# A new order for the head of a hand-written plan: batch 0's second slice and batch 1's last transposed weights ahead of the third slice of G

## The chip, the core and the metric

The kernel runs on one NeuronCore of a Trainium2 chip. The core has five engines with instruction streams of their own: TensorE (PE; its weight loads are a row of their own, PEld), VectorE (DVE), ScalarE (ACT), GpSimd (POOL) and SyncE (SP, which only issues transfers). They meet through semaphores. Transfers run on 16 shared DMA engines; SP, ACT and POOL issue them. The metric is the device time of one execution in microseconds, the median of several runs.

## What is computed

Eight batches of eight heads. Each head has 512 tokens `x` and 32 `state` rows, 64 numbers each. The tokens attend to the states and the states to the tokens; both results, heads side by side, go through a feed-forward layer with a three-way maximum.

```python
scores = scale * np.matmul(x, state.transpose(0, 1, 3, 2))
a = np.exp(scores - scores.max(-1, keepdims=True))
a /= a.sum(-1, keepdims=True) + 1e-09
xread = np.matmul(a, state)
# sread: the same with state and x exchanged
attn = np.concatenate([xread, sread], axis=2)      # 8 x 8 x (512+32) x 64
x = attn.transpose(0, 2, 1, 3).reshape(4352, 512)
h = np.maximum(np.maximum(x @ w1, x @ w2), x @ w3)  # w1, w2, w3: 512 x 768
out = h @ w_out                                     # 768 x 512
```

## The kernel before

**The algebra.** For the tokens of batch b, `xread @ w` is never formed through `xread`. The states of the batch are first multiplied with the three weight matrices, which gives G (line 363: 256 rows of head and state by 3 x 768 columns), and then the attention weights are multiplied with G. So per batch there are: the scores (`sc`), their exponentials (`ex`), row sums (`sum`), the normalised weights `a` (`wt`), their transpose `aT` (`at` and `atc` on TensorE and a copy, or `atd`, a DMA transpose), G in slices (`g`, or runs of columns `gr`) with its evacuation from PSUM to SBUF (`gc`, `grc`), the first layer (`l1`, six blocks m of 128 hidden columns, each with three PSUM banks, one for each of w1, w2, w3, two matmuls into each, line 416), the three-way maximum (`m0` on ACT copies the first bank, `ma` and `mb` on DVE take the maximum with the second and third), and the second layer (`l2`, line 447) with its evacuation (`l2c`) and stores (`so`). `sr` and `srs` are the states' own reading of the tokens and its scaling; `pad` lays x out for it.

**Order.** Nothing is scheduled automatically. A plan of short operations, written out as text, is walked through once, and each operation appends its instructions to the streams of its engines. Within an engine the order of the plan is the order of execution; between engines semaphores hold. `FIRST` holds the head (batches 0 and 1 and the beginning of batch 2), `EACH` one period for batches 2 to 6 with batch numbers relative to the period's, `LAST` the end. The letters behind an operation choose its engine: A ACT, D DVE, P POOL, S SP; `AD` gives one half to each.

**Loads.** `lst k` loads the states of batches 2k and 2k+1; `stc` casts them, `stt` transposes them on TensorE, `stp` places them into the block-diagonal tile `bds[k]`. `lxg b g` loads half of the heads of x of batch b through POOL, which casts on the way; `lxu` loads without a cast (through SP), and `cxu` casts. `lw m0 m1 i` loads columns 128 m0 to 128 m1 of weight matrix i (line 179), `lwo` the output weights (line 184). Slice m of G (`g b m`) needs columns 128 m to 128 m + 128 of all three matrices. `ones` on POOL first copies a number out of the output weights (line 194), so it waits for them. `xtd b` (line 249) is SP's DMA transpose of x for the scores; batches 0 and 1 are transposed on TensorE instead (`xt`, then `xtc`).

**PSUM.** There are four single banks (`BANKS` gives the bank of each use in the plan's order) and two pairs (`PAIRS`). A product may start when the last reader of its bank is done. A slice of G takes a pair, a block of `l1` three of the four single banks.

**Fillers.** `busy n` issues n matmuls of zeros (line 211) that nobody reads. They stand in the head, where TensorE would otherwise wait.

**The part around the change**, TensorE's order before, from the first slices of G on:

```
at 0 0; sr 0; busy; at 0 1; g 0 0; busy; g 1 0; sr 1; at 1 0; g 1 1; g 0 1; l1 0 0; g 1 2; g 0 2; busy;
at 1 1; l1 0 1; l1 0 2; l1 1 0; l1 1 1; g 0 3; g 1 3; stt 1; l1 1 2; g 0 5; g 0 4; l1 0 3; g 1 4;
gr 2 ..; l1 1 3; l1 0 5; gr 2 ..; g 1 5; l1 1 4; gr 2 ..; gr 2 ..; l1 0 4; stt 2; sc 2; l2 0 3; l2 0 1;
```

Of the kernel before, what the change touches and what calls it, by code (L numbers as in the profile page):

```python
# [17 lines left out]
FIRST = """  # L18
    lst 0 A; lxu 0 0 S; zero; clr 0; clr 1; clr 2; clr 3; warm; lxg 0 1; busy 1; xones 1; ident; busy 1;
    lxg 1 0; busy 1; busy 1; stc 0 D; busy 1; busy 1; busy 1; busy 1; busy 1; lxg 1 1; stt 0; busy 2;  # L20
    cxu 0 0 D; xt 0 0; stp 0 A; busy 1; xt 0 1; busy 1; xtc 0 0 D; lw 0 2 1; lw 0 2 2; xtc 0 1 D;
    busy 1; sc 0 0; busy 1; lw 0 1 0; busy 1; sc 0 1; lw 1 3 0; ex 0 0; busy 1; busy 1; xt 1 0; sum 0 0;
    lw 2 3 1; busy 1; ex 0 1; sum 0 1; xt 1 1; busy 1; xtc 1 0 AD; busy 1; lw 2 3 2; busy 1; xtc 1 1 A;
# [14 lines left out]
"""
EACH = """
    pad 1; gr 1 1792 2304; gr 1 0 512; grc 1 1792 2304 AD; l2 -1 0; l2 -1 1; l1 0 0; grc 1 0 512 D;  # L40
    l2c -1 0 A; m0 0 0; sc 1 -; l2 -1 3; gr 1 1024 1280; ex 1 -; xtd 2; gr 1 1280 1792; l2c -1 1 D;
    ma 0 0; gr 1 512 1024; mb 0 0; sr 1; grc 1 1024 1280 A; l1 0 1; l1 0 2; sum 1 -; l1 0 3; srs 1;
    l1 0 5; l2c -1 3 A; m0 0 1; m0 0 2; ma 0 1; mb 0 1; ma 0 2; m0 0 3; mb 0 2; srt -2; ma 0 3;
    wt 1 - P; m0 0 5; mb 0 3; l2 -1 2; grc 1 1280 1792 A; grc 1 512 1024 A; ma 0 5; mb 0 5; l2c -1 2 D;
    l1 0 4; so -1 2 4 P; m0 0 4; ma 0 4; lx 3; mb 0 4; atd 1; ap -2 A; so -1 0 2 P;
"""
LAST = """
    srt 6; l1 7 0; srt 7; l2 6 0; l1 7 2; m0 7 0; l1 7 3; l1 7 4; ap 7 D; m0 7 2; srt 5; ap 6 A; ma 7 0;
    m0 7 3; mb 7 0; ap 5 A; l2c 6 0 D; ma 7 2; l2 6 1; l1s 0; l2 6 2; m0 7 4; mb 7 2; l1 7 1; l2c 6 1 A;
    ma 7 3; m0 s 0; l2c 6 2 A; l1s 2; l1 7 5; ma 7 4; mb 7 4; look; ma s 0; m0 7 1; m0 s 2; mb s 0;  # L50
    so 6 2 3 S; m0 7 5; mb 7 3; l1s 1; ma 7 1; mb 7 1; ma s 2; mb s 2; ma 7 5; m0 s 1; ma s 1; l1s 5;
    so 6 0 1 S; mb 7 5; l2p 7 2 384 512; l1s 3; m0 s 5; ma s 5; mb s 1; m0 s 3; mb s 5;
    l2pc 7 2 384 512 A; l2p 7 0 384 512; l2p 7 3 256 512; sop 7 2 384 512 P; ma s 3; l2p 7 2 128 384;
    mb s 3; l2p 7 0 0 128; l2pc 7 0 0 128 A; l2pc 7 3 256 512 D; l2p 7 1 0 128; l2p 7 3 0 256;
    l2pc 7 0 384 512 D; flag; l2pc 7 1 0 128 A; l2pc 7 2 128 384 A; l1s 4; m0 s 4; l2 6 3;
    sop 7 0 0 128 P; ma s 4; sop 7 0 384 512 P; mb s 4; l2p s 0 256 512; so 6 1 2 P; l2 s 1;
    sop 7 3 256 512 A; l2c 6 3 D; l2p 7 2 0 128; sop 7 1 0 128 S; l2p s 0 0 256; so 6 3 4 A;
# [18 lines left out]
def kernel(  # L76
# [41 lines left out]
    st = [data.tile([128, 4, 2, D], BF16, name=f"st{k}") for k in range(B // 2)]  # L118
# [97 lines left out]
    def states_cast(k, c):  # L216
        copier[c](out=st[k], in_=st_f[k].unsqueeze(2).to_broadcast((128, 4, 2, D)))
# [326 lines left out]
    def perform(plan, base=0):  # L544
        for op in plan.replace("\n", " ").split(";"):
# [132 lines left out]
```

## Time and profile before

| | |
|---|---|
| median of 3 runs | 153.05 us (152.54 to 153.25) |
| the profiled execution, first to last instruction | 151.4 us |
| TensorE busy | 146.4 us, 97% |
| VectorE, ScalarE, GpSimd busy | 118.9, 82.8, 57.0 us |
| fillers on TensorE (line 211) | 27, 10.0 us |
| DMA | 22.29 MB, mean 147 GB/s |

The median lies 1.65 us above the span; that is what lies around the first and the last instruction, and the difference between executions. All times of a profile are counted from the span's first instruction. A busy TensorE isn't TensorE at its peak: matmuls are pipelined and their ends are modelled, so that a group of six that takes 1.3 us at the rate of its starts is shown with up to 1.47 us. A row of a timeline gives the start, the length, the engine, the line, the operation and its tiles, the number of instructions that were merged, and in brackets the idle time of the engine ahead of it with what ended it. `SPq` and `ACTq` rows are issues of transfers.

### The profile page before, as it was taken

What the parts mean: (1) busy time and instruction counts of PE and PEld (TensorE: products, weight loads), DVE (VectorE), ACT (ScalarE), POOL (GpSimd) and SP (SyncE); (2) the same over time, 40 slices, a digit from 0 to 9 for tenths busy, and PEclk for the clock granted to TensorE, in tenths of its full rate; (3) what the DMA queues carried; (4) which work ended last, traced back from release to release, by engine and by line L of the source; (5) the groups of instructions that cost most, each with busy time, mean ns of one, the idle gap of its engine ahead of it and who ended that gap; (6) DMA issues with size and microseconds to landing.
All of it is one profiled execution on the core that took longest, in us unless ns stands there. A gap on an engine that the chain in (4) does not pass through costs nothing.

```text
span 151.4 us, 3635 instructions
## 1 busy us (share of the span) xinstructions
PE 146.4 (97%) x1431; PEld 73.8 (49%) x1431; DVE 118.9 (79%) x204; ACT 82.8 (55%) x143; POOL 57.0 (38%) x79
## 2 busy tenths in 40 slices
PE   6999799999999999999999999999999999999992
PEld 2566343335445443544354435443544446679771
DVE  6477698999977898879987988798879887675353
ACT  3368558976364665466646664666466653331220
POOL 6979650561528505540554046414331200001500
PEclk9999999999999999999999999999999999999999
DMA  3999999979737979999589749974503250300455
GB/s 115 211 189 195 207 198 195 151 149 139 139 74 167 230 59 265 129 223 132 155 124 230 144 130 140 232 122 141 218 0 78 68 226 4 122 18 17 175 180 196
DMA packets 39108, 22.29 MB, mean 147 GB/s; under 512 B 23072, under 2 KB 36896, under 8 KB 39088
## 3 DMA queue, kind: packets, MB, share of 16 engines
q0 software_dynamic: 15872, 13.96, 48.7%
q1 hardware_dynamic: 21776, 6.82, 23.4%
q10 hardware_dynamic: 1440, 1.25, 2.7%
q8 instruction: 12, 0.20, 0.5%
q14 instruction: 8, 0.07, 0.2%
HBM read 15.20 MB, written 8.91 MB: 159 GB/s over the span
## 4 chain that ended last, share of the span: by engine, by line
PE 86%; DMA 6%; POOL 4%; issue 1%; DVE 1%; POOLq 0%
PE pw L416 46%; PE po L447 25%; DMA w<-in_moe_w_dram 6%; PE pg L363 5%; PE po L462 4%; POOL w L179 2%; PE ps L262 2%; PE psr L327 2%; POOL x L168 1%; PE pgh L363 1%; PE pt L222 1%; DVE held L522 0%; PE idle L520 0%; PE idle L211 0%; DVE osb L466 0%
## 5 line engine op out<-in xcount | busy, mean ns | idle before, releaser
L416 PE MATMUL pw<-aT,G 128*128 128x512 bf16 x288 | 66.8, 379 | 0.0
L431 ACT CAST t<-pw 128x512 bf16<-128x512 f32 (+1 forms) x54 | 30.4, 564 | 28.9 <-PE pw L416 27.2
L416 PEld LDWEIGHTS <-G 128*128 128x128 bf16 x288 | 27.2, 98 | 33.2 <-issue 1.9
L436 DVE TENSOR_TENSOR t<-t,pw 128x512 bf16<-128x512 bf16 (+1 forms) x54 | 35.4, 655 | 9.5 <-ACT t L431 7.4
L447 PE MATMUL po<-wout,ht 128*128 128x512 bf16 x168 | 39.9, 379 | 0.0
L440 DVE TENSOR_TENSOR ht<-t,pw 128x512 bf16<-128x512 bf16 x48 | 32.9, 687 | 4.3
L447 PEld LDWEIGHTS <-ht 128*128 128x128 bf16 x168 | 15.3, 98 | 19.0 <-issue 1.7
L284 POOL TENSOR_TENSOR a<-e,rden 128x1024 bf16<-128x1024 bf16 (+1 forms) x9 | 14.5, 1620 | 24.1 <-ACT osb L454 11.1
L477 POOL DMA_DIRECT2D out_dram<-osb x13 | 7.4, 572 | 30.5 <-ACT t L431 27.5
L403 ACT CAST G<-pg 128x1024 bf16<-128x1024 f32 (+1 forms) x17 | 14.3, 875 | 1.3 <-PE pg L363 1.3
L311 POOL COPY xp<-x 128x1024 bf16<-128x1024 bf16 x12 | 12.3, 1062 | 5.5 <-DMA x<-in_x_dram 5.5
L454 DVE COPY osb<-po 128x512 f32<-128x512 f32 x16 | 10.9, 684 | 2.4 <-PE po L447 2.3
L276 DVE TENSOR_REDUCE seen<-e 128x32 f32<-128x1024 bf16 (+1 forms) x10 | 10.0, 999 | 3.6 <-ACT e L269 3.6
L403 DVE CAST G<-pg 128x1024 bf16<-128x1024 f32 (+1 forms) x13 | 12.2, 972 | 0.7 <-ACT G L403 0.7
L454 ACT COPY osb<-po 128x512 f32<-128x512 f32 x13 | 7.7, 593 | 8.9 <-PE po L447 8.9
L269 ACT ACTIVATE e<-ps 128x1024 bf16<-128x1024 f32 (+1 forms) x10 | 8.5, 854 | 6.6 <-PE ps L262 6.4
L363 PE MATMUL pg<-w,bd 64*32 64x512 bf16 (+1 forms) x288 | 10.8, 362 | 0.9 <-DMA w<-in_moe_w_dram 0.9
L211 PE MATMUL idle<-zero 128*128 128x512 bf16 x27 | 10.0, 477 | 1.3 <-DVE zero L187 1.3
L472 POOL DMA_DIRECT2D out_dram<-osb x4 | 2.2, 544 | 19.4 <-ACT osb L466 19.4
L381 ACT CAST G<-pg 128x768 bf16<-128x768 f32 x9 | 7.1, 801 | 3.3 <-PE pg L363 3.1
L416 PE MATMUL pw<-atp,w 128*128 128x256 bf16 x72 | 8.7, 272 | 0.0
L416 PEld LDWEIGHTS <-w 128*128 128x128 bf16 x72 | 6.9, 98 | 1.5
(70 smaller groups left out, 116.0 us busy)
## 6 DMA issues: line engine op xcount, KB each, us to landing
out_dram<-osb POOLq DMA_DIRECT2D x12, 512.0 KB, 3.5
x<-in_x_dram POOLq DMA_DIRECT2D x4, 512.0 KB, 7.3
x<-in_x_dram POOLq DMA_DIRECT2D x7, 256.0 KB, 5.5
w<-in_moe_w_dram POOLq DMA_DIRECT2D x4, 256.0 KB, 7.5
w<-in_moe_w_dram POOLq DMA_DIRECT2D x2, 384.0 KB, 7.9
wout<-in_moe_w_out_dram POOLq DMA_DIRECT2D x1, 768.0 KB, 11.6
out_dram<-osb SPq DMA_DIRECT2D x3, 256.0 KB, 2.4
osb<-in_x_dram SPq DMA_DIRECT2D x1, 512.0 KB, 4.0
```

The source lines that it names most:

```text
L211: nc.tensor.matmul(p, zero[:, 0:128], zero, start=True, stop=True)
L276: nc.vector.reduce_sum(out=den, in_=parity(e[b], g), axis=AX.X)
L284: times[c](out=parity(a[b], g).rearrange("p j g s n -> p j (g s) n"), in0=parity(e[b], g).rearrange("p j g s n -> p j (g s) n"), in1=rdens ...
L311: nc.gpsimd.tensor_copy(out=xp[b][:, :, :, g * (D + 1):g * (D + 1) + D], in_=v[:, g])
L363: nc.tensor.matmul(p(s, g), bd(b, 2 * s + g)[64 * g:64 * g + 64, g, :], f(w_sb[64 * g:64 * g + 64, s]), start=True, stop=True, tile_positi ...
L403: copier[c[g]](out=v[:, g:h], in_=p[:, g:h, 0:c1 - c0])
L416: nc.tensor.matmul(pw[i][:, 0:n], lhs(i, k), rhs(k), start=(k == 0), stop=(k == nk - 1))
L431: nc.scalar.copy(out=t0s[b, m][:, 0:n], in_=open_ps["l", b, m][0][:, 0:n])
L436: nc.vector.tensor_max(t1s[b, m][:, 0:n], t0s.pop((b, m))[:, 0:n], open_ps["l", b, m][1][:, 0:n])
L440: nc.vector.tensor_max(ht[b][:, m, :], t1s.pop((b, m))[:, 0:n], open_ps.pop(("l", b, m))[2][:, 0:n])
L447: nc.tensor.matmul(p, ht[b][:, m, j * 128:(j + 1) * 128], wout_sb[:, m, :], start=(m == 0), stop=(m == NM - 1))
L454: copier[c[i]](out=o[:, j, i * w:i * w + w], in_=p[:, i * w:i * w + w])
```

## The change

**Form.** `FIRST`, `EACH` and `LAST` become one `PLAN` that is written out for all batches. The buffers, which rotated before, are now named by a table (`PLACES`), in the order in which they rotated; a buffer is taken where it is first written. Two buffers hold the cast states instead of four. The four groups of tokens are kept in the order 0, 2, 1, 3 from the exponentials on (`turned`), and the second layer takes its columns accordingly. New functions for transposed scores (`sq`, `eq`, `etd`, `std`) exist but stand nowhere in the plan.

**Order.** From `gr 3 512 1024` on, TensorE's instructions stand in the same order as before, with the same banks but for the first few; so do those of VectorE from `sum 3`, ACT from `gr 3 ..`'s last evacuations, and the rest from batch 4's loads on. What differs is the head:

- TensorE: ten `busy` operations, eleven fillers, fewer. `at 1 1` and `l1 0 1` stand ahead of `g 0 2` and `g 1 2`. The blocks and slices behind them change places.
- ACT and DVE exchange evacuations: `xtc 0`, `gc 0 0`, `atc 1 1`, `gc 0 5`, the run 0 to 512 of batch 2, and batch 0's second-layer evacuations go to ACT; `stp 0`, `gc 0 1`, `wt 0 1`, `wt 2` to DVE; `gc 1 1`, `gc 0 4`, `gc 1 5` and the run 1792 to 2304 are halved between them.
- ACT issues `lst 1` and `lst 2` one behind the other, around `ex 1 1`; `lst 2` stood behind `m0 1 1`.
- POOL's loads of W come in the order `lw 0 2 1; lw 0 1 0; lw 0 2 2; lw 1 3 0; lw 2 3 2; lw 2 3 1; lw 3 6 1; wt 0 0; lw 3 4 0; lw 3 6 2; wt 1 0; wt 1 1; lw 4 6 0` (before `lw 0 2 1; lw 0 2 2; lw 0 1 0; lw 1 3 0; lw 2 3 1; lw 2 3 2; wt 0 0; wt 0 1; lw 3 4 0; lw 3 6 2; lw 3 6 1; lw 4 6 0; wt 1 1`). Behind them: `stc 1; lxg 2 0; lxg 2 1; lwo; stc 2; ones; pad 2; lxg 3 1; stc 3; lxg 3 0; pad 3; so 0 0` (before `stc 1; lxg 2 1; lxg 2 0; lwo; pad 2; ones; stc 2; lxg 3 1; lxg 3 0; stc 3; wt 2; so 0 0; lx 4; so 0 2; pad 3`).
- SP: `atd 2` stands ahead of `xtd 3`.

The core of the diff (of the plan, the part of the new head that the text speaks of):

```diff
-    busy 1; wt 0 0 P; wt 0 1 P; xones 0; sc 1 0; ex 1 0; busy 1; sc 1 1; at 0 0; atc 0 0 A; sr 0;
-    busy 1; sum 1 0; lw 3 4 0; at 0 1; lst 1 A; lw 3 6 2; lw 3 6 1; ex 1 1; wt 1 0 D; g 0 0; gc 0 0 D;
-    busy 1; sum 1 1; g 1 0; sr 1; atc 0 1 A; lw 4 6 0; wt 1 1 P; at 1 0; srs 0; g 1 1; g 0 1; stc 1 P;
-    l1 0 0; gc 1 1 D; gc 1 0 A; g 1 2; g 0 2; atc 1 0 A; busy 1; gc 0 1 A; m0 0 0; at 1 1; lxg 2 1;
-    srs 1; ma 0 0; l1 0 1; lxg 2 0; gc 0 2 A; l1 0 2; atc 1 1 D; l1 1 0; m0 0 1; m0 0 2; lwo; m0 1 0;
+    ex 1 0; busy 1; busy 1; sc 1 1; lst 1 A; lw 1 3 0; ex 1 1; lst 2 A; lw 2 3 2; lw 2 3 1; lw 3 6 1; wt 0 0 P;
+    wt 0 1 D; lw 3 4 0; at 0 0; sr 0; at 0 1; atc 0 0 A; sum 1 0; sum 1 1; lw 3 6 2; wt 1 0 P; g 0 0; g 1 0;
+    wt 1 1 P; sr 1; atc 0 1 A; gc 1 0 D; lw 4 6 0; at 1 0; srs 1; srs 0; gc 0 0 A; stc 1 P; lxg 2 0; lxg 2 1;
+    lwo; g 0 1; g 1 1; atc 1 0 A; l1 0 0; stc 2 P; ones; pad 2; at 1 1; m0 0 0; gc 0 1 D; ma 0 0; gc 1 1 AD;
+    atc 1 1 A; l1 0 1; g 0 2; g 1 2; m0 0 1; mb 0 0; ma 0 1; l1 1 0; xtd 2; lst 3 S; mb 0 1; gc 0 2 A; m0 1 0;
+    ma 1 0; mb 1 0; l1 0 2; gc 1 2 A; m0 0 2; ma 0 2; mb 0 2; l1 1 1; g 1 3; m0 1 1; ma 1 1; mb 1 1; g 0 3;
+    stt 1; l1 1 2; gc 0 3 A; gc 1 3 A; stp 1 D; m0 1 2; ma 1 2; g 0 4; g 0 5; gc 0 4 AD; mb 1 2; gc 0 5 A;
+    l1 0 3; m0 0 3; ma 0 3; g 1 4; gr 2 1792 2304; l1 1 3; gc 1 4 A; grc 2 1792 2304 AD; m0 1 3; gr 2 0 512;
+    g 1 5; mb 0 3; ma 1 3; grc 2 0 512 A; gc 1 5 AD; mb 1 3; l1 0 5; gr 2 1280 1792; gr 2 512 1024; m0 0 5;
+    ma 0 5; mb 0 5; l1 1 4; m0 1 4; ma 1 4; grc 2 1280 1792 AD; l1 0 4; m0 0 4; ma 0 4; stt 2; sc 2 -; mb 0 4;
+    ex 2 -; stp 2 A; l2 0 1; mb 1 4; l2c 0 1 A; sum 2 -; l2 0 3; l1 1 5; l2c 0 3 A; lxg 3 1; m0 1 5; stc 3 P;
+    wt 2 - D; lxg 3 0; stt 3; ma 1 5; grc 2 512 1024 A; mb 1 5; l2 0 2; stp 3 A; l2c 0 2 A; atd 2; xtd 3;
...
+    def buffer(shape, dtype, tag, key, name=None):
+        n = places[tag][str(key)] if places else str((B if key == "s" else key) % 2)
+        return work.tile(shape, dtype, tag=tag + n, bufs=1, name=name or tag)
...
     def exps(b, g=None):
-        nc.scalar.activation(out=parity(e[b], g), in_=open_ps.pop(("s", b, g)), func=AF.Exp, scale=scale)
+        new(e, b, [128, J, 2, HS, Ns], "e")
+        nc.scalar.activation(
+            out=parity(e[b], g).rearrange("p (c i) g s n -> p i c (g s n)", i=2),
+            in_=open_ps.pop(("s", b, g)).rearrange("p (i c) g s n -> p i c (g s n)", i=2),
+            func=AF.Exp, scale=scale)
...
-            nc.tensor.matmul(p, ht[b][:, m, j * 128:(j + 1) * 128], wout_sb[:, m, :],
+            nc.tensor.matmul(p, ht[b][:, m, tokens(b, j)], wout_sb[:, m, :],
```

More of the change, by code (lines that the diff above doesn't have):

```diff
@@ L38 @@
[L38 to L45, printed above, removed]
@@ L117 @@
     st_f = [data.tile([128, 4, D], F32, name=f"stf{k}") for k in range(B // 2)]
-    st = [data.tile([128, 4, 2, D], BF16, name=f"st{k}") for k in range(B // 2)]
+    st = {}
     bds = [data.tile([128, 2, H, 2, Ns], BF16, name=f"bd{k}") for k in range(B // 2)]
@@ L241, in x_turned @@
     def x_turned(b, g, c):
+        new(xT, b, [128, H, 2, 128], "xT")
         p, w = open_ps.pop(("x", b, g)), HS // len(c)
@@ L306, in pad @@
     def pad(b):
-        xp[b] = work.tile([128, HS, J, 2 * D + 2], BF16, tag="xp", name="xp")
+        new(xp, b, [128, HS, J, 2 * D + 2], "xp")
         nc.gpsimd.memset(xp[b][:, :, :, D:D + 1], 1.0)
```

241 lines of the change are left out of this document (147 added, 94 removed), and 3 rows, old and new, of the table BANKS.

## The prediction

> **What bounds the kernel now.** I read the chain of waits on the page first, then the same chain in order of time, then busy time by stretches, then the timeline of each engine around the edit.
>
> ```profile
> PE 86%; DMA 6%; POOL 4%; issue 1%; DVE 1%; POOLq 0%
> ```
>
> ```profile
> 8.17 9.70 DMA w<-in_moe_w_dram
> 17.86 0.04 issue
> 17.91 0.52 PE pg L363 x16
> 18.43 0.32 PE idle L211
> 18.75 0.22 PE pat L295 x4
> 18.97 5.20 PE pw L416 x24
> ...
> 35.51 0.47 PE ps L262 x16
> ...
> 148.99 0.69 DVE held L522
> ```
>
> The chain in order of time (start, length, what) has one load of W up to 17.86 us and almost nothing but TensorE behind it. That load is W2's third slice, columns 256 to 383 (`lw 2 3 2`), which both products `g 1 2` and `g 0 2` need.
>
> ```profile
> 13.00:17.90 4.90, 4.05 (x80) 1.93 (x78) 4.74 (x11) 3.51 (x6) 3.40 (x5) 1.00 1.54 204
> 17.90:35.30 17.40, 17.39 (x169) 7.02 (x170) 15.36 (x24) 12.93 (x20) 7.71 (x13) 1.00 1.20 171
> 48.00:148.00 100.00, 100.00 (x920) 51.49 (x917) 79.28 (x137) 52.95 (x95) 29.62 (x36) 1.00 0.61 137
> ```
>
> Columns: stretch, length, busy time and count of PE, weight loads, DVE, ACT, POOL, then granted clock, DMA share, GB/s. From 17.90 on TensorE has no gap, and the work behind 35.3 us is the same before and after, in nearly the same order. So the edit is worth what it moves the start of batch 2's scores (`sc 2`, first matmul at 35.35), less what it loses between there and about 49 us. Before 35 us VectorE is nearly full too (15.36 of 17.40, and 1.14 of the rest is one wait, below): TensorE can't run ahead of it for free.
>
> **The change, part by part.** First the stretch up to the load.
>
> ```profile
> 1.27 4.02 PE L211 MATMUL idle<-zero 128*128 128x512 bf16 x9 [1.27 <-DVE zero L187]
> ...
> 13.35 0.36 PE L363 MATMUL pg<-w,bd 64*32 64x384 bf16 x8
> ...
> 15.58 1.47 PE L416 MATMUL pw<-aT,G 128*128 128x512 bf16 x6
> 17.91 0.52 PE L363 MATMUL pg<-w,bd 64*32 64x384 bf16 x16 [0.86 <-DMA w<-in_moe_w_dram]
> ...
> 35.35 0.63 PE L262 MATMUL ps<-bd,xT 128*128 128x64 bf16 x16
> ```
>
> ```profile
> 10.04 2.05 POOL L284 TENSOR_TENSOR a<-e,rden 128x512 bf16<-128x512 bf16 x2 [1.10 <-DVE rden L278]
> ```
>
> ```profile
> 13.22 0.69 DVE L284 TENSOR_TENSOR a<-e,rden 128x512 bf16<-128x512 bf16 x1
> 13.83 0.95 DVE L381 CAST G<-pg 128x768 bf16<-128x768 f32 x1
> ...
> 15.72 0.29 DVE L343 TENSOR_TENSOR sr<-psr,seen 128x128 bf16<-128x128 f32 x1
> ...
> 17.20 0.68 DVE L436 TENSOR_TENSOR t<-t,pw 128x512 bf16<-128x512 bf16 x1
> 19.01 0.42 DVE L298 COPY aT<-pat 128x512 bf16<-128x512 bf16 x1 [1.14 <-PE pat L295]
> ```
>
> ```profile
> 15.23 0.59 ACT L298 COPY aT<-pat 128x512 bf16<-128x512 bf16 x1
> 15.72 0.80 ACT L381 CAST G<-pg 128x768 bf16<-128x768 f32 x1
> 16.41 0.60 ACT L431 CAST t<-pw 128x512 bf16<-128x512 f32 x1
> ```
>
> `g 0 0` keeps its place, about 13.3: the bytes queued ahead of its weights are the same. Its weights `a 0 1` move from POOL (two in 2.05) to VectorE (0.69), so ACT has copied both halves of `aT 0` by about 13.75 and evacuates `g 0 0` by 13.75 + 0.80 = 14.55. VectorE evacuates `g 1 0` (product done about 14.05) by 14.05 + 0.95 = 15.0. The next two products reuse those PSUM pairs: `g 0 1` at 14.65, `g 1 1` at 15.1, and `l1 0 0` starts at about 15.4 (15.58 before). Then comes what is new: `at 1 1` (0.22, its `a 1 1` on POOL is no longer last in the queue) at 16.7 and `l1 0 1` (6 matmuls, 5.20/4 = 1.30) at 16.95. Is its input there? VectorE: `g 1 0` to 15.0, two scalings of some 0.35 (0.29 and a reciprocal), then `gc 0 1` of 0.95: 16.65, a margin of 0.3. Its three banks come free by `m0 0 0` (16.0 + 0.60), `ma 0 0` (16.65 + 0.68) and the copy of `at 1 1` (17.1 + 0.59), each about when its turn comes. So `l1 0 1` ends at 18.25 and the third slice starts at 18.3 if its weights are there.
>
> Are they? The last of the three is now `lw 2 3 1`, behind the same bytes. But `lst 2`, issued at 23.33 before, now leaves ACT directly behind `lst 1`, about 12.5.
>
> ```profile
> stf<-in_state_dram ACTq DMA_DIRECT2D x1, 128.0 KB, 5.4
> ```
>
> ```profile
> 23.33 0.34 ACTq L152 DMA_DIRECT2D stf<-in_state_dram  x1
> ```
>
> It brings 128 KB into a stretch that moves 204 GB/s: 131/204 = 0.64 us if W has to make room for all of it. So the third slice starts between 18.3 (nothing lost) and 17.9 + 0.64 + 0.1 = 18.6. I take 18.4. [...]
>
> Before, the point "third slice, `at 1 1` and `l1 0 1` done" is 18.97 + 1.30 = 20.27. After it is 18.4 + 0.52 = 18.9. Gain there 1.35 (1.15 to 1.45): the wait of 0.86, the filler of 0.32, and a slightly earlier `l1 0 0`. The other ten fillers removed lie in waits ahead of 15 us and cost nothing on the path: TensorE's dates there are set by x, W and the copies.
>
> From there to `sc 2` the same products run in a new order. VectorE gives up two whole evacuations (`gc 0 5`, the run 0 to 512) and one copy, and takes four halves (`gc 1 1`, `gc 0 4`, the run 1792 to 2304, `gc 1 5`) and half a placing: even, within one evacuation. VectorE itself starts its pairs earlier, since its wait of 1.14 at 19.01 goes. ACT is the tighter one: four times a first bank is freed by an `m0` (0.60) that stands behind an evacuation (0.80), ahead of `l1 0 3`, `l1 1 3`, `l1 0 5` and `l1 1 4`, 0.1 to 0.2 each by the same walk: 0.4 to 0.8. TensorE thus reaches `sc 2` between 35.35 - 1.45 + 0.4 = 34.3 and 35.35 - 1.15 + 0.8 = 35.0. I take 34.5.
>
> **What is late next.** `sc 2` reads `xT 2`, a DMA transpose on SP.
>
> ```profile
> 26.38 4.75 SPq L249 DMA_TRANSPOSE xT<-x  x1
> ```
>
> ```profile
> DMA to landing us min/median/max: 8.3/8.3/8.3
> ```
>
> ```profile
> 26.35 2.05 POOL L311 COPY xp<-x 128x1024 bf16<-128x1024 bf16 x2 [5.51 <-DMA x<-in_x_dram]
> ...
> 31.42 0.19 POOL L194 COPY last<-wout 128x1 bf16<-128x1 bf16 x1 [3.02 <-DMA wout<-in_moe_w_out_dram]
> ```
>
> ```profile
> 29.00:30.00 1.00, 1.00 (x7) 0.41 (x5) 0.90 (x2) 1.00 (x3) 0.00 (x0) 1.00 1.19 63
> 30.00:31.00 1.00, 1.00 (x6) 0.45 (x5) 0.90 (x3) 1.00 (x2) 0.00 (x0) 1.00 0.44 22
> 31.00:32.00 1.00, 1.00 (x19) 0.25 (x18) 1.00 (x3) 0.32 (x1) 0.58 (x3) 1.00 1.17 263
> ```
>
> It landed at 26.38 + 8.3 = 34.7, only 0.65 ahead of its use. It crawled while `wout` was in flight (63 and 22 GB/s in all) and ran once that had landed at 31.4 (263). The bytes queued up to `wout`'s end are the same after the change, so `xT 2` again lands at 34.7, and one weight load later `sc 2` starts at 34.8. The cap binds: the gain shrinks from 0.85 (35.35 - 34.5) to 0.55.
>
> Behind it, `wt 2` moves from POOL to VectorE and POOL's queue turns round: `ones`, which waits for `wout`, now stands ahead of `pad 2` and of both loads of x 3.
>
> ```profile
> 32.25 1.50 POOL L168 DMA_DIRECT2D x<-in_x_dram  x2
> ...
> 34.91 0.62 POOL L217 CAST st<-stf 128x512 bf16<-128x512 f32 x1 [1.15 <-DMA stf<-in_state_dram]
> ```
>
> ```profile
> 37.76 1.80 SPq L249 DMA_TRANSPOSE xT<-x  x1
> 41.60 1.23 SPq L302 DMA_TRANSPOSE aT<-a  x1
> ```
>
> ```profile
> DMA to landing us min/median/max: 4.3/4.3/4.3
> ```
>
> `pad 2` runs 31.8 to 33.85, the first x 3 load follows, `stc 3` waits for its states to 34.9 and ends at 35.5, the second load is issued then; before, the second of the pair, issued at 33.0, had landed when the transpose left at 37.76, so 4.7 at most, and it lands by 40.2. SP sends `atd 2` first: about 39.4 + 1.23. `xtd 3` then goes at 40.7 and lands at 45.0, for a `sc 3` at 47.56 - 0.55 = 47.0: two us of cover. A few banks are tight behind `sc 2` (`l1 1 5` on `l2c 0 1`, `l2 0 2` on `m0 1 5`, `sc 3` on an evacuation): 0 to 0.2, I take 0.05. Sum: 0.55 - 0.05 = 0.5 off the profiled execution's span of 151.4, which lies 1.65 under the median of 153.05. Forecast: 153.05 - 0.5 = **152.55 us**.
>
> **The rivals.**
> 1. *The transpose isn't the cap.* If `xT 2` lands by 34.2, TensorE's own arrival decides: 34.3 to 34.5, a gain of 0.85 to 1.05, and with ACT's waits hidden, 1.35: 151.7 to 152.2. For it: the data could all have gone by 33 at the rate of the 31 to 32 stretch. Against it: it had that rate before and landed at 34.7.
> 2. *The transpose moves with its input.* `lst 2` ahead of x 2 delays its landing from 26.3 to 26.95; with the same 8.3 it lands at 35.25 and `sc 2` starts at 35.35, as before: 153.05, or 152.9 to 153.3 with the tight banks. For it: the input is what releases SP. Against it: the crawl until `wout` landed.
> 3. *Slower, by x 3.* POOL's new queue puts `wout`'s landing, `pad 2`, two loads and SP's `atd 2` in a row ahead of `xT 3`. It decides when that lands past 47.0. If the transpose meets loads and stores as `xT 2` did and takes 8.3, it lands at 40.7 + 8.3 = 49.0: 2.0 us late, time 152.55 + 2.0 = 154.6. For it: batch 0's stores leave POOL about then. Against it: 4.3 in the quiet stretch.
> 4. *The wait only changes its name.* If `gc 0 1` slips by 0.9 on VectorE, TensorE stands ahead of `l1 0 1` as long as it stood for W: no gain, 153.0.
> 5. *The clock falls.* Eleven fillers go. The first nine went at 4.02/9 = 0.45 us each, the later one in the chain at 0.22 to 0.32; a stretch as long as that first one at half pace in the saturated part costs about 2: 155. [...]
>
> **How the numbers follow.** Forecast 0.36 (152.3 to 152.8); rival 1 0.24; rival 2 0.18; rival 3 0.15; rival 4 0.05; rival 5 0.02. The range reaches over the forecast and rivals 1, 2 and 4, 151.5 to 153.5, and leaves out 0.17. A difference of 0.5% is 0.77 us, about what can be told from no change: faster than 152.28 are rival 1 and a quarter of the forecast's share, 0.24 + 0.08 = 0.32; slower than 153.82 are rivals 3 and 5 with 0.01 of rival 2, 0.18; the rest, 0.50, within.
>
> **What would show it.** Right: no wait for W at the third slice, `l1 0 1` ahead of it, it starting at 18.3 to 18.6; `sc 2` released by `xT 2`, about 34.8; 0.5 less at every later mark. Wrong: a wait for W still there; `sc 2` before 34.4 or after 35.3; a TensorE wait for `xT 3`; a VectorE or ACT wait ahead of `l1 0 1`.

## The result, and the profile after

| | kernel before | changed kernel |
|---|---|---|
| median of the runs, same chip | 152.75 us (152.25 to 153.25, 12 runs) | 153.78 us (153.07 to 154.31, 12 runs) |
| ratio | | 1.0065, 95% interval [1.0047, 1.0083] |
| profiled execution, first to last instruction | 151.4 us | 152.3 us |

The changed kernel is 1.0 us slower, outside the predicted range. The page of after, its chain of waits by engine:

```profile
PE 93%; DVE 2%; ACT 2%; issue 1%; DVEq 0%
```

The 6% of DMA are gone from the chain: no load of W is on the path any more. ACT and DVE have taken its place. TensorE's timeline of after, in which the places that the prediction dated stand (start, length, engine, line, tiles, number merged, idle time ahead):

```profile
6.16 1.06 PE L277 MATMUL pxt<-ident,x 128*128 128x128 bf16 x8
...
16.08 1.47 PE L476 MATMUL pw<-aT,G 128*128 128x512 bf16 x6
...
17.61 1.50 PE L476 MATMUL pw<-aT,G 128*128 128x512 bf16 x6
19.03 0.52 PE L426 MATMUL pg<-w,bd 64*32 64x384 bf16 x16
...
36.04 0.63 PE L304 MATMUL ps<-bd,xT 128*128 128x64 bf16 x16
48.25 0.63 PE L304 MATMUL ps<-bd,xT 128*128 128x64 bf16 x16
```

The third slice (19.03) follows `l1 0 1` (17.61) without a wait for W, as meant. But `l1 0 0` starts at 16.08 (15.4 was predicted, 15.58 before), and `sc 2` at 36.04, 0.69 later than before (35.35). From there on nothing differs: `sc 3` follows 12.21 behind, as before (47.56 - 35.35). The loss lies ahead of `sc 2`, part of it after the third slice, as the chain of after in order of time shows:

```profile
19.55 3.99 PE pw L476 x18
...
28.75 0.60 ACT G L465
...
29.38 0.70 DVE G L465
...
30.12 0.57 PE pg L426 x16
...
36.20 0.47 PE ps L304 x16
```

The point "third slice, `at 1 1` and `l1 0 1` done" is at 19.55, 0.72 ahead of before's 20.27; then 16.65 us pass to `sc 2`, where before took 15.24 (35.51 - 20.27). In the middle stands one evacuation in two halves, ACT's 0.60 and then VectorE's 0.70, one behind the other. The waits of after between 17 and 37 us, of VectorE and of TensorE (who waited for whom, us in total, times, longest):

```profile
DVE G L443 <- ACT G L443: 0.8, 1, 0.8
DVE G L465 <- ACT G L465: 0.7, 1, 0.7
...
PE pg L426 <- DVE G L465: 0.5, 1, 0.5
PE pg L426 <- DVE G L443: 0.2, 1, 0.2
PE pw L476 <- DVE ht L504: 0.2, 1, 0.2
```

VectorE stands 0.8 and 0.7 us in front of its half of an `AD` evacuation until ACT has finished the other; TensorE then waits for the pair that it frees. None of TensorE's waits here is for ACT. Last, the transposes of x, by their tile, between 28 and 52 us:

```profile
L290 SPq DMA_TRANSPOSE xT<-x x2: 1757/3560/5364, 25.8 to 42.2; - x2
...
DMA to landing us min/median/max: 6.0/7.1/8.2
```

Issued at 25.8, `xT 2` lands 8.2 later at 34.0, two us ahead of its use: it is no cap. Issued at 42.2, `xT 3` lands 6.0 later at 48.2, just before its use (48.25).

### The profile page after: what moved, and what is told of

It is laid out like the page before. It is cut to its first block, busy times and chain, and to the rows that moved or that the text cites. A ratio compares the mean times of both kernels' runs of the same rounds, so it can differ in the third digit from the quotient of the medians.

```text
span 152.3 us, 3602 instructions
## 1 busy us (share of the span) xinstructions
PE 144.9 (95%) x1406; PEld 73.0 (48%) x1420; DVE 117.2 (77%) x203; ACT 85.4 (56%) x148; POOL 55.3 (36%) x78
## 4 chain that ended last, share of the span: by engine, by line
PE 93%; DVE 2%; ACT 2%; issue 1%; DVEq 0%
PE pw L476 46%; PE po L513 25%; PE pg L426 6%; PE po L531 4%; PE idle L248 4%; PE ps L304 2%; PE psr L390 2%; ACT xT L285 1%; PE pxt L277 1%; PE pgh L426 1%; PE pt L260 1%; PE pat L357 1%; DVE G L465 0%; DVE held L592 0%; DVE ht L504 0%
## 5 line engine op out<-in xcount | busy, mean ns | idle before, releaser
L513 PE MATMUL po<-wout,ht 128*128 128x512 bf16 x155 | 39.2, 379 | 0.7
L348 POOL TENSOR_TENSOR a<-e,rden 128x1024 bf16<-128x1024 bf16 (+1 forms) x8 | 12.6, 1583 | 22.2 <-ACT osb L525 11.4
L465 ACT CAST G<-pg 128x1024 bf16<-128x1024 f32 (+1 forms) x20 | 17.4, 899 | 1.6 <-PE pg L426 1.6
L525 ACT COPY osb<-po 128x512 f32<-128x512 f32 x15 | 8.8, 592 | 6.8 <-PE po L513 6.8
L525 DVE COPY osb<-po 128x512 f32<-128x512 f32 x14 | 9.6, 687 | 3.8 <-PE po L513 3.7
L248 PE MATMUL idle<-zero 128*128 128x512 bf16 x15 | 7.2, 536 | 2.7 <-DVE zero L224 1.3
L465 DVE CAST G<-pg 128x512 bf16<-128x512 f32 (+1 forms) x10 | 8.6, 897 | 1.1 <-ACT G L465 1.1
L443 ACT CAST G<-pg 128x768 bf16<-128x768 f32 (+1 forms) x10 | 6.9, 708 | 1.7 <-PE pg L426 1.7
L216 POOL DMA_DIRECT2D w<-in_moe_w_dram x10 | 7.6, 782 | 0.0
```

The costliest lines, as they stand in the source:

```text
L248: nc.tensor.matmul(p, zero[:, 0:128], zero, start=True, stop=True)
L348: times[c](out=parity(a[b], g).rearrange("p j g s n -> p j (g s) n"), in0=parity(e[b], g).rearrange("p j g s n -> p j (g s) n"), in1=rdens ...
L465: copier[c[g]](out=v[:, g:h], in_=p[:, g:h, 0:c1 - c0])
L513: nc.tensor.matmul(p, ht[b][:, m, tokens(b, j)], wout_sb[:, m, :], start=(m == 0), stop=(m == NM - 1))
L525: copier[c[i]](out=o[:, j, i * w:i * w + w], in_=p[:, i * w:i * w + w])
```

## The experiments

The main numbers of all runs, in one table. "Pace" is that of batch 0's first eight transposes of x (full: 0.61 to 0.65 us, half: 1.06, and in e7 1.84 for the sixteen of both parts).

| run | ratio to the kernel before | pace | sc 2 | sc 3 behind it |
|---|---|---|---|---|
| before | 1 | full | 35.35 | 12.21 |
| after | 1.0065 [1.0047, 1.0083] | half | 36.04 | 12.21 |
| e1 after again | 1.0058 [1.0037, 1.0079] | full | 35.25 | 12.22 |
| e2 before, exchange alone | 1.0081 [1.0056, 1.0106] | full | 35.84 | 12.21 |
| e3 whole evacuations | 1.0023 [1.0004, 1.0042] | full | 34.91 | 12.22 |
| e4 pairs mirrored | 1.0003 [0.9982, 1.0023] | half | 35.47 | 12.23 |
| e5 before again | 0.9996 [0.9966, 1.0025] | full | 34.28 | 12.21 |
| e6 both of these | 1.0032 [1.0007, 1.0056] | half | 35.69 | 12.21 |
| e7 transposes first | 1.0041 [1.0009, 1.0073] | half | 35.17 | 12.59 |
| e8 e6, e7 and `pad 2` | 1.0022 [0.9996, 1.0048] | full | 34.55 | 12.40 |
| e9 pairs, x 3 first | 1.0037 [1.0014, 1.0059] | half | 35.46 | 12.61 |
| e10 pairs, transposes, x 3 | 1.0002 [0.9976, 1.0027] | full | 34.77 | 12.21 |
| e11 whole, transposes, x 3 | 1.0022 [0.9994, 1.0051] | full | 34.57 | 12.21 |
| e12, e13, e14 before, one execution each | | full | 34.19, 35.96, 35.44 | 12.21 |
| e15 before, one filler less | 0.9972 [0.9947, 0.9997] | full | 33.93 | 12.34 |
| e16 before, three fillers less | 0.9973 [0.9952, 0.9993] | full | 34.69 | 12.35 |
| e17 after, two fillers more | 1.0064 [1.0038, 1.0090] | full | 35.54 | 12.21 |

The theory after the result: there was less to win than one execution of before showed, and the new order loses more up to `sc 2` than was counted, by evacuations in series and by a later start. The rivals: the clock, batch 3's x, or the exchange of the title itself.

**The kernel before, again (e5, e12, e13, e14).** Nothing is edited.

> The kernel before, one more profile. Its wait for W's third slice rested on one profiled execution. If the late landing belongs to the order of the loads, the slice again starts at 17.8 to 18.1 us behind a DMA wait of 0.6 to 1.0 us. If it was an accident of that execution, the slice lands by 16.5 us and no DMA wait stands there. Scores of batch 2 at 34.8 to 35.4 us in either case, since the median of the kernel before lies 0.3 us under that first profile.

> The kernel before, one look. My theory (the wait for W belonged to one execution): the third slice's weights land before 16.9 us, the slice follows l1 0 0 without a DMA wait, the span is 150.3 to 151.2 us. Rival (the wait is there in most executions): a wait of 0.4 to 0.9 us, the slice at 17.3 to 18.0, span 151.0 to 151.9.

> As e12, a second look: no DMA wait at the third slice by my theory, 0.4 to 0.9 us by the rival.

> As e12, a third look: no DMA wait at the third slice by my theory, 0.4 to 0.9 us by the rival. If the looks differ among themselves, the share of those that wait, times the wait, is what the change had to win.

How long the last two loads of W took, from issue (8.1 to 8.6 us holds the third slice's last) to landing, in the first profile of before and then in e5:

```profile
DMA to landing us min/median/max: 7.8/8.8/9.7
```

```profile
DMA to landing us min/median/max: 7.7/7.7/7.7
```

Issued at the same time, the load took 9.7 in the one execution and 7.7 in the other. TensorE waits for W at the third slice in one of the five profiled executions of before; in e5, e12, e13 and e14 the weights are there. So for the wait on W the theory holds: on average the exchange had some 0.86/5 = 0.17 us of it to win. What held that one load up for 2 us isn't settled. But in e13 and e14 the slice itself stops, by 0.33 and 0.34 us, ahead of its last three products. TensorE's timeline of e14:

```profile
18.18 0.34 PE L363 MATMUL pg<-w,bd 64*32 64x384 bf16 x3 [0.34 <-issue]
```

"issue" means that the profile shows nothing it waited for. `l1 0 1` starts 1.56 and 1.58 behind the slice in e13 and e14, where it takes 0.90 in e12. No profiled execution with the new head has a stop of that size there. What causes it, and whether the new order avoids it, is open; counted with the wait for W, there were (0.86 + 0.66 + 0.68)/5 = 0.44 us to win instead of 0.17. e13 shows one more accident, of TensorE's timeline:

```profile
10.69 0.62 PE L237 MATMUL pxt<-ident,x 128*128 128x128 bf16 x8 [0.56 <-DMA x<-in_x_dram]
```

There batch 1's x came late, and all behind it with it; e14 has a smaller delay of the same kind. Their one timed run each took 153.97 and 153.44 us; e12, without any of these accidents, 152.14. Over these three executions the kernel before spreads by 1.83 us, the two longer ones with a late load and a stop.

**The changed kernel again (e1).** Nothing is edited.

> The changed kernel once more, as the base for the others. If its loss stands in the instruction order, it is again 0.4 to 0.9% slower than the kernel before, and its profile has again VectorE waiting about 1.4 us for ACT's halves (lines 443 and 465) between 28 and 33 us and the scores of batch 2 at 36.0 +- 0.3 us. If the loss was one bad execution (a late load, a late clock), the profile shows the scores of batch 2 by 35.0 us.

TensorE's timeline of e1:

```profile
5.83 0.62 PE L277 MATMUL pxt<-ident,x 128*128 128x128 bf16 x8 [0.20 <-DVE x L213]
...
15.29 1.47 PE L476 MATMUL pw<-aT,G 128*128 128x512 bf16 x6
```

The first transposes run at full pace, and `l1 0 0` starts at 15.29 instead of 16.08, 0.79 earlier. `sc 2` at 35.25 lies between the two expected dates: after's late start explains 0.79 of its 36.04, and the loss in ratio stays. The waits for halves are the same as in after. So e1 and e12 are the executions to compare, each without an accident, though on different chips (on the chips used, the kernel before took between 152.66 and 152.92 in the median). Their chains in order of time, e12 and then e1:

```profile
16.82 0.45 PE pg L363 x16
17.26 0.32 PE idle L211
17.59 0.22 PE pat L295 x4
17.81 5.20 PE pw L416 x24
...
34.35 0.47 PE ps L262 x16
```

```profile
18.31 0.48 PE pg L426 x16
18.79 3.99 PE pw L476 x18
...
27.97 0.60 ACT G L465
...
28.59 0.70 DVE G L465
...
35.41 0.47 PE ps L304 x16
```

The point "third slice, `at 1 1`, `l1 0 1` done" is at 17.81 + 1.30 = 19.11 in e12 and at 18.79 in e1: the head wins 0.32. From there to `sc 2` it is 15.24 and 16.62: 1.38 lost. The sum, 1.06 slower at `sc 2`, is close to the 1.03 of the medians; e12 and e1 themselves lie 0.6 and 0.4 under theirs. Busy time in that stretch, by the timeline's own dates, which make the loss 1.29 and the head's gain 0.23, e12 and then e1 (stretch, length, then PE, weight loads, DVE, ACT, POOL):

```profile
18.95:34.19 15.24, 15.24 (x144) 6.00 (x143) 14.34 (x22) 11.54 (x18) 5.74 (x10) 1.00 1.22 188
```

```profile
18.72:35.25 16.53, 15.62 (x150) 6.33 (x143) 14.23 (x24) 12.05 (x20) 7.70 (x14) 1.00 1.09 160
```

VectorE's load is the same (14.34 and 14.23). TensorE is idle for 0.91 (the waits of 0.5, 0.2 and 0.2), and its busy time is drawn out by 0.38. The blocks of `l1` are not what is drawn out: by the rows' starts, the waits left out, they take 8.37 in e1 and 8.32 in e12. TensorE's timelines of the runs of batch 2, first before (the same spacing as in e12) and then e1:

```profile
28.64 2.79 PE L416 MATMUL pw<-aT,G 128*128 128x512 bf16 x12
31.36 0.57 PE L363 MATMUL pg<-w,bd 64*32 64x512 bf16 x16
...
33.26 0.62 PE L363 MATMUL pg<-w,bd 64*32 64x512 bf16 x16
33.82 1.47 PE L416 MATMUL pw<-aT,G 128*128 128x512 bf16 x6
```

```profile
27.35 1.47 PE L476 MATMUL pw<-aT,G 128*128 128x512 bf16 x6
29.33 0.57 PE L426 MATMUL pg<-w,bd 64*32 64x512 bf16 x16 [0.52 <-DVE G L465]
...
31.24 0.41 PE L426 MATMUL pg<-w,bd 64*32 64x512 bf16 x8
31.85 0.41 PE L426 MATMUL pg<-w,bd 64*32 64x512 bf16 x8 [0.20 <-DVE G L443]
32.44 2.75 PE L476 MATMUL pw<-aT,G 128*128 128x512 bf16 x12 [0.18 <-DVE ht L504]
```

In e1 the block at 27.35 and the wait behind it take 1.98, where one block with nothing behind it takes 1.40; the two runs at 31.24 take 1.20, where before takes 0.56 (33.26 to 33.82). That is 0.58 + 0.64 = 1.22 of the 1.29, at two places, and at both TensorE stands for VectorE's half of an evacuation or for what VectorE does behind it. The rows show a second thing that the new order changed. Before has two blocks of `l1` (twelve matmuls, 2.72) between the run 1792 to 2304 and the run 0 to 512; the new order has one, since `l1 0 5` went behind. So an evacuation there has one block less to hide behind, halved or whole. No run here puts `l1 0 5` back, so this part is argued and not shown.

**The exchange of the title alone (e2)**, made on the kernel before (what the title calls batch 0's second slice is its second block of the first layer, `l1 0 1`; the second line of each pair is shown in part):

```diff
-    l1 0 0; gc 1 1 D; gc 1 0 A; g 1 2; g 0 2; atc 1 0 A; busy 1; gc 0 1 A; m0 0 0; at 1 1; lxg 2 1;
-    srs 1; ma 0 0; l1 0 1; lxg 2 0; gc 0 2 A; l1 0 2; atc 1 1 D; l1 1 0; m0 0 1; m0 0 2;
+    l1 0 0; gc 1 1 D; gc 1 0 A; atc 1 0 A; busy 1; gc 0 1 A; m0 0 0; at 1 1; lxg 2 1;
+    srs 1; ma 0 0; l1 0 1; g 1 2; g 0 2; lxg 2 0; m0 0 1; gc 0 2 A; l1 0 2; atc 1 1 D; l1 1 0; m0 0 2;
```

> The kernel before with only the titled exchange: the third slice of G (both batches) behind the transpose of batch 1's last weights and batch 0's second block, and the copy m0 0 1 ahead of the evacuation of that slice; no letter, bank or load changed. If the wait for W was worth its 0.86 us and the exchange covers it, the third slice starts at 18.6 to 19.4 us without a DMA wait, the scores of batch 2 come 0.5 to 0.9 us earlier (34.5 to 34.9 us) and the time falls by 0.3 to 0.6%. If VectorE and ACT, not W, set the pace behind the slice, the DMA wait goes and the scores of batch 2 stay at 35.2 to 35.5 us: same time within 0.2%.

TensorE's timeline of e2:

```profile
20.61 1.69 PE L416 MATMUL pw<-aT,G 128*128 128x512 bf16 x7 [0.93 <-ACT G L381]
```

Slower, 1.0081, which neither expected outcome had. The slice and the block that reads it, `l1 0 2`, are now neighbours, and TensorE waits 0.93 for the slice's evacuation. In the kernel before `at 1 1` and `l1 0 1` stood between them and covered it; the changed kernel puts `l1 1 0` there. The exchange doesn't stand by itself: it needs the reordering that comes with it.

**Evacuations (e3, e4, e6).** e3 puts five evacuations back on the engine that had them before: four that were halved become whole, and the run 0 to 512 goes from ACT to VectorE (only the operations that differ are shown):

```diff
-    gc 1 1 AD;  gc 0 4 AD;  grc 2 1792 2304 AD;  grc 2 0 512 A;  gc 1 5 AD;
+    gc 1 1 D;   gc 0 4 A;   grc 2 1792 2304 A;   grc 2 0 512 D;  gc 1 5 A;
```

e4 leaves them halved and exchanges the two PSUM pairs (0 for 1) from `gr 2 0 512` on. In the changed kernel that run takes the pair of `gr 2 1792 2304` just ahead of it, whose halves are still under way. e6 makes both edits.

> The changed kernel with the engine letters of five evacuations put back as before: gc 1 1 whole on VectorE, gc 0 4 and gc 1 5 and the run 1792 to 2304 whole on ACT, the run 0 to 512 whole on VectorE. If the serial halves are the loss (the VectorE half starts when the ACT half ends, two stalls of 0.66 and 0.76 us), those stalls go, the scores of batch 2 come 0.7 to 1.4 us earlier (34.6 to 35.3 us) and the time is 0.4 to 0.9% below the changed kernel's. If the pairs are the loss (the run 0 to 512 reuses the pair of the run just before it), TensorE still waits about 0.5 us ahead of the run 0 to 512, now for a whole evacuation on ACT, and the time stays within 0.2% of the changed kernel's or gets worse.

> The changed kernel with the two PSUM pairs exchanged from the run 0 to 512 of batch 2 on, as the kernel before had it there: the run 0 to 512 takes the pair that gc 1 4 frees, and slice 5 of batch 1 takes the pair of the run 1792 to 2304, one product later; everything behind is mirrored. If the pairs are the loss, TensorE's wait of 0.52 us ahead of the run goes, and the scores of batch 2 come 0.4 to 0.9 us earlier. If the serial halves are the loss, VectorE still waits 0.6 to 0.8 us at each half of the run 1792 to 2304 and of gc 1 5, and the scores of batch 2 stay at 35.8 to 36.1 us.

> The changed kernel with both edits: five evacuations whole as before, and the pairs as before from the run 0 to 512 on. If the two are one loss seen from two sides (the pair that comes free late, through a serial half), the sum is like the better of the two: 0.2 to 0.5% under the changed kernel. If they are two losses, TensorE and VectorE have no waits above 0.2 us between 28 and 33 us, the scores of batch 2 come 1.0 to 1.5 us before the changed kernel's at the same clock, and the time is 0.6 to 0.9% under the changed kernel's, below or level with the kernel before.

The half on VectorE in after and the whole on ACT in e5, each from its engine's timeline:

```profile
29.38 0.69 DVE L465 CAST G<-pg 128x512 bf16<-128x512 f32 x1 [0.66 <-ACT G L465]
```

```profile
28.75 1.02 ACT L403 CAST G<-pg 128x1024 bf16<-128x1024 f32 x1
```

Two halves in series take 0.60 + 0.70 = 1.30 and keep both engines; the whole takes 1.02 of one. e3 wins 0.34 at `sc 2` (35.25 to 34.91, both at full pace), e4 0.57 (36.04 to 35.47, both at half pace), e6 only 0.35 (36.04 to 35.69). By the ratios, against those of e1 and after, e3 wins 0.35% to 0.42% and e4 0.55% to 0.62%, that is 0.5 to 0.65 and 0.85 to 0.95 us. The two don't add up, and e6's timeline shows what is in the way:

```profile
32.28 0.63 PE L426 MATMUL pg<-w,bd 64*32 64x512 bf16 x16 [0.40 <-DVE G L465]
```

There TensorE waits for VectorE's whole evacuation of the run 0 to 512, which takes 1.22. From the point used above (third slice, `at 1 1`, `l1 0 1` done) to `sc 2`, by the timelines' dates, e3, e4 and e6 still take 16.08, 15.98 and 16.19, where e1 takes 16.53, after 16.56 and e12 15.24. So the halves and the pairs are shown to be part of the loss, by these profiles 0.35 to 0.6 us of 1.3; the rest is still there in all three. That e4's time is nevertheless level with that of the kernel before (1.0003) fits the accidents in the latter's runs.

**The head's transposes (e7, e17).** e7 puts them ahead of their fillers, their copies whole on VectorE and `stp 0` on ACT:

```diff
-    stp 0 D; clr 3; busy 1; busy 1; xt 0 1; xtc 0 0 A; xtc 0 1 AD; sc 0 0; busy 1; sc 0 1;
+    stp 0 A; clr 3; xt 0 1; xtc 0 0 D; xtc 0 1 D; busy 1; sc 0 0; busy 1; busy 1; sc 0 1;
```

> The changed kernel with the first transposes as before: stp 0 whole on ACT, xtc 0 0 and xtc 0 1 whole on VectorE, and the two fillers between xt 0 0 and xt 0 1 moved behind xt 0 1. If the head's transposes, not W, now set the start of the first block (16.1 us in the profile with the late clock, 15.3 with an early one), batch 0's second scores start by 8.8 us instead of 9.1 to 9.9, the first block by 15.3 us, and the time falls 0.2 to 0.5% below the changed kernel's, with less spread between executions. If W or VectorE sets it, the first block stays where it was and the time is within 0.2%.

TensorE's timeline of e7, and what its weight loads waited for between 45 and 52 us:

```profile
15.21 1.47 PE L473 MATMUL pw<-aT,G 128*128 128x512 bf16 x6
```

```profile
PEld L301 <- DMA xT<-x: 0.7, 1, 0.7
```

At half pace too `l1 0 0` starts at 15.21 and not at 16.08, and `sc 2` 0.87 earlier (35.17). But `sc 3` now waits for `xT 3` and comes 12.59 behind instead of 12.21: 0.38 of it goes there.

The pace itself: with the new head five of ten profiled executions (after, e4, e6, e7, e9) run the first transposes at half pace; with the old one none of eight (the first, e2, e5, e12 to e16) does. The spans of after's twelve runs lie in two groups, six at 151.3 to 151.8 and six at 152.1 to 152.4; whether the groups are the two paces isn't shown, since the kernel before spreads as widely (150.4 to 151.8 in e1's comparison) with no half pace in any profile. The granted clock of the profile reads 1.00 from 4 to 8 us in after as in e1, so it doesn't show the difference either. e17 brings the fillers ahead of `stt 0` back from seven to nine, their banks in turn as before:

> The changed kernel with two more fillers ahead of `stt 0`, nine as in the kernel before, their banks taken in turn as there. My theory: TensorE's load between 1.3 and 5 us decides whether the full clock comes at about 5 or at about 7.6 us; with the old load it comes at about 5 in nearly every execution, so the spans of the timed runs lose their upper group (152.1 to 152.4; the lower lies at 151.3 to 151.8), the first eight transposes of x take 0.62 us in the profile, and the ratio to the kernel before falls from 1.0065 to 1.003 to 1.005. Rival (the moment is given by something that the load does not touch): both groups stay, ratio 1.006 to 1.007.

Its profile shows full pace, and of eight spans six lie at 151.4 to 151.9. But the ratio stayed at 1.0064: `l1 0 0` starts at 15.57, since the two fillers themselves come first. The ratio didn't fall as the theory had it, and this decides nothing on the cause; and the pace isn't what makes the kernel slow: e1 at full pace is 1.06 behind e12.

**Batch 3's x (e8 to e11).** e8 is e6 and e7 with `pad 2` ahead of `ones`; e9 is e4, e10 is e4 and e7, e11 is e3 and e7, each with this:

```diff
-    stc 2 P; ones; pad 2;
+    stc 2 P; pad 2; ones;
...
-    lxg 3 1; m0 1 5; stc 3 P; wt 2 - D; lxg 3 0;
+    lxg 3 1; lxg 3 0; m0 1 5; stc 3 P; wt 2 - D;
...
-    atd 2; xtd 3;
+    xtd 3; atd 2;
```

> The changed kernel with the edits of the two runs ahead of this one together, and pad 2 ahead of ones in POOL's queue, so that x 3 is loaded about 2 us earlier. If the losses add up, the third slice starts at 18.0 to 18.4 us and the scores of batch 2 at 33.5 to 34.4 us, 0.6 to 1.4% under the changed kernel and 0.2 to 0.8% under the kernel before. If the transpose of x 2 is the cap that was forecast, the scores start when it lands, 32.6 to 34.7 us in the profiles so far, with a TensorE wait on it.

> The changed kernel with the mirrored pairs, and batch 3's x brought forward: `pad 2` ahead of `ones`, `lxg 3 0` directly behind `lxg 3 1`, SP's `xtd 3` ahead of `atd 2` as in the kernel before. My theory: in the run with the mirrored pairs alone the scores of batch 3 waited 0.4 us for xT 3, so this takes that wait away and makes it faster by 0.2 to 0.4 us: 152.5 to 152.8 us, ratio 0.998 to 1.001, no wait for xT 3, and from the first matmul of sc 2 to TensorE's last instruction 113.2 us or a little less. Rival (xT 3 lands just when it is needed and hides nothing; or the loads brought forward slow xT 2): 152.9 to 153.3.

> The same, and the head's transposes of x put first (`xt 0 1` ahead of the two fillers, both copies whole on VectorE, `stp 0` on ScalarE). The version with these transposes alone won 0.9 us up to l1 0 0 and gave 0.9 us back to xT 3 (PEld L301 and PE ps L301 waited 0.7 and 0.2 us). My theory: with xT 3 no longer late the gain stays: sc 2 at 34.3 to 34.8, from there 113.2 us, 152.0 to 152.5 us, ratio 0.995 to 0.998: faster than both kernels. Rival (the edits are one loss seen from several sides, some other bound, such as VectorE's load up to sc 2 or xT 2's landing, takes over): 152.7 to 153.4, sc 2 not before 35.

> The same as the run before it, but with the five evacuations whole instead of the mirrored pairs. My theory: whole evacuations end 0.3 us later than halves on one engine but start the other engine's next instruction at once; they alone were worth 0.35% against 0.5% for the pairs, so 0.1 to 0.3 us slower than the run before it: 152.2 to 152.8 us. Rival (halves in series are the larger loss): faster than the run before it.

e8 misses its expectation: `sc 2` comes at 34.55 instead of by 34.4, `sc 3` 0.19 late with a wait for `xT 3`, and the ratio stays above 1. In e9 the wait for `xT 3` is gone, and yet `sc 3` comes 12.61 behind `sc 2`: 0.4 lost in another place, and the expectation missed. VectorE's timeline of e4, then those of VectorE and GpSimd of e9:

```profile
38.96 1.23 DVE L348 TENSOR_TENSOR a<-e,rden 128x1024 bf16<-128x1024 bf16 x1
```

```profile
38.96 2.12 DVE L348 TENSOR_TENSOR a<-e,rden 128x1024 bf16<-128x1024 bf16 x1
```

```profile
37.97 2.04 POOL L374 COPY xp<-x 128x1024 bf16<-128x1024 bf16 x2 [1.66 <-DMA x<-in_x_dram]
```

With x 3 there earlier, `pad 3` runs on GpSimd at the same time as `wt 2` on VectorE, and `wt 2` takes 2.12 instead of 1.23. In e4 the same copy starts at 40.32, behind it. TensorE waits for VectorE at that place in e9 (0.23 at 41.73). e10's profile has a wait further on, for batch 3's `aT`, in TensorE's waits between 44 and 70 us:

```profile
PE pw L473 <- DMA aT<-a: 0.7, 1, 0.7
```

But this execution is the slowest of e10's twelve (153.93 us, median 152.80), and e11's, with `sc 2` at 34.57, goes on from there as before, with no such wait. So it isn't shown that this wait belongs to the kernel. By its time e10 is level with the kernel before (1.0002) and misses its expectation, and none of these versions beats the kernel before.

**Fillers (e15, e16).** What is left of the change's gain is the filler that it takes out behind the third slice. e15 takes that one out of the kernel before, with its bank; e16 also the two around the first slice (shown for e15, a part of the line):

```diff
-    g 1 2; g 0 2; atc 1 0 A; busy 1; gc 0 1 A;
+    g 1 2; g 0 2; atc 1 0 A; gc 0 1 A;
```

> The kernel before without the `busy 1` behind `g 0 2`, which stood at 17.30 us in an execution whose W was in time, between the third slice (16.84) and at 1 1 (17.52). My theory: there it lies on TensorE's path, since nothing waited ahead of it, so 0.22 us less: ratio 0.998 to 0.9995, 152.45 to 152.7 us beside 152.75. Rival (VectorE, 14.2 of 15.1 us busy up to sc 2, takes it back): 1.000.

> The same, and without the fillers ahead of at 0 1 and between g 0 0 and g 1 0. My theory: the first of them lies in the wait for W's first slice (landed 13.07, g 0 0 at 13.21) and is worth nothing, the second at most 0.2 us, so 0.2 to 0.4 us less than the kernel before in all: ratio 0.997 to 0.999. Rival (all three hide in waits or are taken back by VectorE): 1.000.

TensorE's timeline of e15:

```profile
16.69 0.54 PE L343 MATMUL pg<-w,bd 64*32 64x384 bf16 x16
...
17.40 3.83 PE L396 MATMUL pw<-aT,G 128*128 128x512 bf16 x17
```

`at 1 1` follows the slice directly, and `l1 0 1` starts 0.71 behind the slice's start, where the same timeline of e12 has 0.90 (16.75 and 17.65). `sc 2` comes at 33.93, 0.26 ahead of e12's. But by batch 4's scores this execution has lost it again (61.77 beside e12's 61.65), so the gain shows in the times and not in these two profiles. e15 takes 152.20 us beside 152.87 (medians), ratio 0.9972 [0.9947, 0.9997]: it beats both kernels, by little. e16 wins no more, 0.9973, which fits that the other two fillers lie in waits.

## Why the prediction was wrong

- **What bounds it**: right. TensorE's work behind `sc 2` takes the same time in all these kernels where nothing new waits there, and the changed kernel is decided by its `sc 2`.
- **"The wait of 0.86"**: the mechanism was right, the size was not. The wait is gone, but it belonged to one execution in five of the kernel before; it was taken for a property of the kernel. Worth 0.17 on average, at most 0.44 with the unexplained stops of e13 and e14, where 0.86 was summed.
- **"The filler of 0.32"**: right in kind: e12's chain has 0.32, e15's `l1 0 1` comes 0.19 sooner behind the slice, and e15's time is 0.28% [0.03%, 0.53%] shorter. **"A slightly earlier `l1 0 0`"**: nothing, 15.29 (e1) beside 15.35 (e12). So the gain at that point, predicted as 1.35, is 0.32 between executions without an accident; in after itself 0.72, since after's head ran 0.79 late and before's had its wait.
- **From there to `sc 2`, 0.4 to 0.8 lost**: the step that failed most, measured 1.38, and not by the mechanism forecast. The forecast had TensorE wait for ACT's `m0` at four blocks; its measured waits (0.5, 0.2 and 0.2) are all for VectorE. "VectorE: even, within one evacuation" is right as a sum (14.23 beside 14.34) and says nothing of when: the four halves were costed at half a price each, as if the two engines worked side by side. At the two halves that VectorE waited for (0.66 and 0.76) they ran in series, and the pair of the run 1792 to 2304 stayed taken for 1.30 instead of 1.02. The row for this stood on the page of before, in the groups (line 403, idle 0.7 us ahead of it, for ACT's half):

```profile
L403 DVE CAST G<-pg 128x1024 bf16<-128x1024 f32 (+1 forms) x13 | 12.2, 972 | 0.7 <-ACT G L403 0.7
```

- **The cap `xT 2`**: false. It landed at 34.0 and `sc 2` starts at 36.04; TensorE's own arrival decides, as in rival 1, but later. The narrow margin of 0.65 was that of one execution too: in e5 `xT 2` lands at 31.5 (25.3 + 6.2), 2.8 ahead of its use at 34.28, and e12, e13 and e14 show no wait for it.
- **The rivals**: 2 fell with the cap. 3, slower by batch 3's x, named the right queue: `xT 3` lands at 48.2 in after and at 45.9 in e1, where 45.0 was forecast; it costs `sc 3` nothing in either, and e7, whose `sc 2` is earlier, loses 0.38 to it. 4 didn't happen in after; e2 shows its mechanism one slice further on. 5, whose chance was an estimate: no later loss of pace shows, but in half of the profiled executions with the new head the first transposes ran at half pace, 0.8 us at `l1 0 0` that the sentence "the other ten fillers cost nothing" left out; e17 didn't show that the fillers are the cause.

Two slips in the working change nothing: 35.35 - 1.35 + 0.6 is 34.6 and not 34.5, and a quarter of 0.36 is 0.09 and not 0.08. The sum as it should have stood, between executions without an accident: 0.32 won, 1.38 lost, 1.06 slower. What stays open: what delayed that load of W by 2 us, what stops the third slice in e13 and e14, what sets the pace at the start, and how much of the 1.38 is the one block that the new order took from between the runs.

## What to carry to other kernels

Before a wait for a load is worth removing, look at a second and a third profile: a wait that stands on the path of one execution may be absent from the others, as this one was from four of five. The same holds for a margin (0.65 us in the first, 2.8 in e5), and for a wait found after the change. When an evacuation is split between two engines, look in the profile whether the second half waits for the first; here it did, the pair was held for 1.30 us instead of 1.02, and equal sums of VectorE's busy time (14.23 and 14.34) hid it. Count, too, how many products stand between two uses of a bank. This head, with TensorE and VectorE nearly full (15.24 and 14.34 of 15.24 us in e12), handed each gain to the next thing that was just in time, in turn, in the profiled executions, a PSUM pair (0.5 us in e1), a transpose (0.7 in e7), a copy on GpSimd (0.23 in e9) and another transpose (0.7 in e10): the only win in time was an instruction taken off the path with nothing moved (e15, 0.9972).

## What the runs showed of the hardware

- VectorE's scaling `a<-e,rden` took 1.23 us alone (e4) and 2.12 us while GpSimd copied x (e9); GpSimd's two copies took 2.04 in both. In after and e10, where the two also ran at the same time, the scaling took 1.23 and 1.43 and the copies 2.42 and 3.04. Why the one or the other is drawn out, no run here shows.
- The pace of TensorE's first products differs between executions of one kernel: eight transposes at about 6 us took 1.06 us in after and 0.62 in e1. In e1 the full pace is there at 4.8 us (four transposes of the states from 4.81 in 0.38, in after from 4.88 in 0.63), in after only at 7.9 (the next eight of x from 7.91 in 0.61); the granted clock of both profiles reads 1.00 there, and no run here shows the cause.
- With the same issues one load of W took 9.7 us in one execution (the first of before) and 7.7 in another (e5).
- The two engines' halves of one evacuation ran one behind the other (0.60 on ACT, then 0.70 on VectorE, in after), where the whole took 1.02 on ACT and 1.22 on VectorE (e5).
